# Agent attention and a gated feed-forward on one core: all products on two 64-row tiles of the matrix array, each with its own bank

## The chip, the cores and the metric

The kernel runs on one NeuronCore of a Trainium2 chip. The metric is the device time of one execution in microseconds (us). TensorE (PE in the profile) multiplies, ScalarE (ACT) and VectorE (DVE) read and write its result banks and do all elementwise work, GpSimd (POOL) and SyncE (SP) mostly issue transfers.

## What is computed

```python
def sm(a, b):                       # softmax of scaled products
    s = scale * (a @ b.transpose(0, 2, 1))
    s = s - s.max(-1, keepdims=True)
    e = np.exp(s)
    return e / (e.sum(-1, keepdims=True) + 1e-09)
agent_v = sm(agents, k) @ v         # 4 batches, 12480 keys, 49 agents, 128 channels
x = sm(q, agents) @ agent_v         # 49920 tokens, 128 channels
h = x @ w_in                        # w_in 128 x 2048
out = (h * (1 / (1 + np.exp(-1.702 * h)))) @ w_out
```

All data are float32. The weights arrive as 64-bit words and are turned into float32 on DVE.

## The kernel before

**Precision.** A product in full float32 is replaced by products of parts: each operand is split into a high part and the rest. The feed-forward uses float32r parts and drops the product of the two rests, so each product is three. The scores use three bf16 parts and six products.

**Work of one group.** The tokens are cut into 100 chunks of 500, two chunks to a group, 50 groups. `query_scores` multiplies the queries of a group with the 49 agents, a softmax follows, and `query_pairs` transposes its result. The second attention product is folded into the weights: per batch, `weights_part` makes `agent_v @ w_in`, so that the feed-forward takes the 49 softmax rows as its input. A group then has 16 steps, one for each 128 of the 2048 hidden features; `two_steps` records two steps at a time, 400 times in all.

**Up.** The softmax rows are held packed: 49 high rows, 49 rest rows and 30 of the 49 high rows again make 128 rows (`sa`, `sb`, one for each chunk), the remaining 19 rows lie apart in `rq`. So `up` issues four products on the whole array (L438: two hidden blocks by two chunks) and four on 32-row tiles of it (L441, 19 rows each), all into the four banks of `ph`. Eight small transfers for each group and up to six for each weight part (`move`) put the rows where this packing wants them.

**Gelu and split.** ACT applies the activation to each `ph` bank (L451). `high` makes the float32r part `gh`, by a casting transfer from POOL (L457), on ACT (L461) or, once in a group, on DVE (L459); `low` takes the rest on DVE (L466).

**Down.** Four steps later (`LAG = 4`) `down` multiplies with the second matrix (L476): three products for each of two chunks, each over 128 rows of the array, into the two banks of `po`, one for each chunk. After 16 steps `store` copies the banks out on ACT (L487) and SP sends them to memory.

**Order.** PE, ACT, DVE and POOL run in the order in which the program records them (`manual_schedule`). The skeleton of `two_steps`, with t an even step:

```python
g[t], g[t + 1] = up(...)          # PE, ACT
jobs(t)                           # attention work that is due at t
gh[t], gh[t + 1] = high(...)      # POOL, ACT or DVE
down(u = t - 3); second(t); down(u = t - 4)   # second(): jobs(t + 1), then one low()
if last step of the po banks: store(...)
```

Attention work is put at fixed steps: `query_pairs` at 4, `query_scores` at 12, the exponentials of the softmax at 0, key scores of the next batch (39 times in all) and its value products (39 times) at steps between. It has banks of its own, `ps_m`.

Of the kernel before, what the change touches and what calls it, by code (L numbers as in the profile page):

```python
# [8 lines left out]
F32 = mybir.dt.float32  # L9
# [10 lines left out]
KB = 8  # L20
# [17 lines left out]
R = 30  # L38
WORDS_USED = (3, 7, 11)
BOTH = (0,)  # L40
ON_DVE = (2,)
# [6 lines left out]
def kernel(  # L48
# [33 lines left out]
    ps_m = ctx.enter_context(tc.tile_pool(name="ps_m", bufs=2, space=bass.MemoryType.PSUM))  # L82


# [41 lines left out]
    def to_float32(w, out=None):  # L126
# [12 lines left out]
        m = work.tile([P, 512], U32, name="m21", tag="o")  # L139
# [50 lines left out]
    def scores(b, parts, ps, c):  # L190
        x0, x1, x2 = parts
        for j in range(c * KB // 2, (c + 1) * KB // 2):
            t = slice(j * TB, j * TB + P)
            o = ps[:, j * A : (j + 1) * A]
            products = [(x0, 0), (x0, 1), (x0, 2), (x1, 0), (x1, 1), (x2, 0)]
            for i, (x, y) in enumerate(products):
                nc.tensor.matmul(  # L197
                    out=o,
                    lhsT=x[:, t],
                    rhs=ag_part[:, b, y, :],  # L200
                    start=(i == 0),
                    stop=(i == len(products) - 1),
                )


    def score_halves(n, parts, c):
        x0, x1, x2 = parts
        b = chunk(n, c)[0]
        a = ag_part[:, b].rearrange("p i a -> p (i a)")
        mm = nc.tensor.matmul  # L210
        ps = ps_m.tile([P, 512], F32, name="ps_m")
        for j in range(KB // 2):
            t0 = (c * KB // 2 + j) * QB
            t = slice(t0, t0 + P)
            o = ps[:, j * 2 * A : (j + 1) * 2 * A]
            mm(out=o, lhsT=x0[:, t], rhs=a[:, 0 : 2 * A], start=True, stop=False)  # L216
            mm(out=o[:, A:], lhsT=x0[:, t], rhs=a[:, 2 * A :], start=False, stop=False)
            mm(out=o, lhsT=x1[:, t], rhs=a[:, 0 : 2 * A], start=False, stop=False)  # L218
            mm(out=o[:, 0:A], lhsT=x2[:, t], rhs=a[:, 0:A], start=False, stop=True)  # L219
        return ps[:QB, : KB * A].rearrange("p (j i a) -> p j a i", i=2, a=A)  # L220

    def score_bank():
        ps = ps_m.tile([P, 512], F32, name="ps_m")
        return ps, ps[:TB, : KB * A].rearrange("p (j a) -> p j a", a=A)
# [7 lines left out]
    def first_key_scores(g, kt):  # L232

        for c in range(2):
            ps = ps_m.tile([P, 512], F32, name="ps_m")
# [19 lines left out]
    def key_store(g, s):  # L255
        nc.scalar.copy(out=score[:TB, g * KB : (g + 1) * KB, :], in_=s)

# [5 lines left out]
    def key_max_1(d):  # L263
        mx = d["mx"]
        ps = ps_m.tile([P, 512], F32, name="ps_m")
# [3 lines left out]
        mrow = work.tile([P, TB], F32, name="mrow", bufs=1)  # L269
# [3 lines left out]
    def key_max_2(d):  # L273
        mrow = d["mrow"]
        ps = ps_m.tile([P, 512], F32, name="ps_m")
        nc.tensor.transpose(out=ps[:TB, :A], in_=mrow[:A], identity=ident[:A, :A])
        nc.vector.tensor_copy(out=max_b[:TB], in_=ps[:TB, :A])
# [31 lines left out]
    def key_matmuls(g, ps, first, last):  # L309
        for j in range(KB):  # L310
            nc.tensor.matmul(  # L311
                out=ps[:, : 2 * C + 2],
                lhsT=e_pair[g % 2][:TB, j, :],
                rhs=v_pair[:TB, j, :],
                start=(first and j == 0),
                stop=(last and j == KB - 1),
            )

    def key_values(g):
        ps = ps_m.tile([P, 512], F32, name="ps_m")  # L320
        key_matmuls(g, ps, True, True)
        return ps

    def key_sum(g, ps, acc):
        if g == 0:
            nc.vector.tensor_copy(out=acc, in_=ps[:, : 2 * C + 1])
        else:
            nc.vector.tensor_add(out=acc, in0=ps[:, : 2 * C + 1], in1=acc)


    def weights_0(acc, w):
        zc = work.tile([P, P], F32, name="zc", bufs=1)
        nc.vector.tensor_copy(out=zc, in_=acc[:, 2 * C : 2 * C + 1].broadcast_to([P, P]))
        w["acc"], w["zc"] = acc, zc

    def weights_1(w):
        ps = ps_m.tile([P, 512], F32, name="ps_m")
        nc.tensor.matmul(out=ps[:, 0:P], lhsT=w["acc"][:, 0:C], rhs=sel, start=True, stop=False)
        nc.tensor.matmul(out=ps[:, 0:P], lhsT=w["acc"][:, C : 2 * C], rhs=sel, start=False, stop=True)
        nc.tensor.matmul(out=ps[:, P : 2 * P], lhsT=w["zc"], rhs=sel, start=True, stop=True)  # L340
        rz = work.tile([P, P], F32, name="rz", bufs=1)
# [9 lines left out]
    def weights_part(b, w, c):  # L351
        if c == 0:
            wts[b] = wpool.tile([P, F], F32R, name="wh"), wpool.tile([P, F], F32R, name="wq")
        wh, wq = wts[b]
        s = slice(c * 512, (c + 1) * 512)
        pw = ps_m.tile([P, 512], F32, name="ps_m")
        nc.tensor.matmul(out=pw, lhsT=w["avT"], rhs=w_in_sb[:, s], start=True, stop=True)  # L357
        nc.scalar.copy(out=wh[:, s], in_=pw)
        wl = work.tile([P, 512], F32R, name="wl")
        nc.vector.tensor_sub(out=wl[:A], in0=pw[:A], in1=wh[:A, s].bitcast(F32))  # L360
        move(wh[A:H, s], wl[0 : R // 2])
        move(wh[H + A : P, s], wl[R // 2 : R])
# [489 lines left out]
```

## Time and profile before

| | |
|---|---|
| median of 3 runs | 1993.88 us (1993.75 to 1993.92) |
| profiled execution: its time | 1994.44 us |
| its span, first to last instruction | 1992.6 us |
| PE, DVE, ACT, POOL busy | 1954.5, 1628.2, 1425.9, 260.9 us |
| granted TensorE clock, mean | 0.990 |

Busy shares are means over the span. Matmuls overlap in the array, so their rows are best read by their starts: the distance from one start to the next is what a product costs. In the rows below `x2` joins two instructions that follow each other.

### The profile page before, as it was taken

Reading aid. Unit: us, or ns where it says so; the run is one execution under the profiler, and the core shown is the slowest. Engines: PE = TensorE matmul, PEld = TensorE weight load, DVE = VectorE, ACT = ScalarE, POOL = GpSimd, SP = SyncE. Lnnn points to the kernel's source line nnn. Section 1 sums busy time; section 2 is a strip of 40 time slices with the busy share of each in tenths; the row PEclk is TensorE's granted clock in tenths of the full one; section 3 lists DMA queues with packets and bytes.
Section 4 is the critical chain, followed back from the end, with each engine's and each line's share of the span. In section 5 each row is a group of like instructions: output and inputs, shape, how many; then the busy total and the mean of one; then the engine's idle time right before and its main releaser. Section 6 shows DMA issues by size and latency. Waiting matters only on the chain.

```text
span 1992.6 us, 33879 instructions
## 1 busy us (share of the span) xinstructions
PE 1954.5 (98%) x12462; PEld 1472.6 (74%) x12462; DVE 1628.2 (82%) x2081; ACT 1425.9 (72%) x2364; POOL 260.9 (13%) x597
## 2 busy tenths in 40 slices
PE   7799999999999999999999999999999999999999
PEld 7577777777777777777777777777777777777776
DVE  6689989988788889888878888988877767777775
ACT  3367777777767776777777777677677787777875
POOL 1111111111111111111111111111111111111111
PEclk8899999999999999999999999999999999999999
DMA  9556666566556665665546566565455454554543
GB/s 302 146 172 191 186 192 181 174 185 189 164 181 200 181 182 179 196 183 171 182 160 197 183 204 180 174 191 177 158 163 170 162 181 157 171 165 163 181 145 134
DMA packets 126537, 356.26 MB, mean 179 GB/s; under 512 B 15984, under 2 KB 54752, under 8 KB 126372
## 3 DMA queue, kind: packets, MB, share of 16 engines
q0 software_dynamic: 66080, 234.78, 35.9%
q1 hardware_dynamic: 60292, 119.33, 21.6%
q8 instruction: 98, 1.61, 0.3%
q14 instruction: 67, 0.55, 0.1%
HBM read 81.01 MB, written 25.56 MB: 53 GB/s over the span
## 4 chain that ended last, share of the span: by engine, by line
PE 88%; issue 6%; DVE 3%; DMA 1%; POOL 1%; ACT 1%; POOLq 0%; ACTq 0%; SPq 0%; DVEq 0%
PE po L476 52%; PE ph L438 17%; PE ph L441 8%; PE ps_m L197 2%; PE ps_m L311 2%; PE ps_m L411 1%; PE po L610 1%; PE ps_m L237 1%; PE ps_m L216 1%; PE ps_m L218 1%; DMA gh<-g 1%; DVE gl L466 1%; POOL gh L457 1%; PE ps_m L357 1%; PE ps_m L219 0%
## 5 line engine op out<-in xcount | busy, mean ns | idle before, releaser
L451 ACT ACTIVATE g<-ph 128x500 f32<-128x500 f32 x1600 | 811.1, 593 | 469.8 <-PE ph L441 463.5
L466 DVE TENSOR_TENSOR gl<-g,gh 128x1000 fp32r<-128x1000 f32 x800 | 940.1, 1196 | 129.6 <-DMA gh<-g 83.1
L476 PE MATMUL po<-gh,wo_h 128*128 128x500 f32 x1600 | 532.7, 414 | 0.0
L476 PE MATMUL po<-gl,wo_h 128*128 128x500 f32 x1600 | 494.7, 390 | 4.2 <-DVE gl L466 4.0
L476 PE MATMUL po<-gh,wo_l 128*128 128x500 f32 x1600 | 493.2, 389 | 0.0
L457 POOL DMA_DIRECT2D gh<-g x450 | 241.0, 535 | 1652.7 <-ACT g L451 1053.3
L476 PEld LDWEIGHTS po<-gl,wo_h 128*128 128x128 f32 x1600 | 300.3, 188 | 70.5 <-DVE gl L466 9.3
L476 PEld LDWEIGHTS po<-gh,wo_l 128*128 128x128 f32 x1600 | 301.9, 189 | 62.1
L476 PEld LDWEIGHTS po<-gh,wo_h 128*128 128x128 f32 x1600 | 272.4, 189 | 86.5 <-issue 55.1
L438 PE MATMUL ph<-sa,wh 128*128 128x500 f32 x800 | 315.8, 395 | 2.3 <-DMA wh<-wl 1.6
L461 ACT CAST gh<-g 128x1000 fp32r<-128x1000 f32 x300 | 309.5, 1032 | 8.8
L438 PE MATMUL ph<-sb,wh 128*128 128x500 f32 x800 | 314.7, 393 | 0.0
L441 PE MATMUL ph<-rq,wq 19*128 19x500 f32 x1600 | 201.5, 491 | 0.2 <-DMA wq<-wl 0.2
L438 PEld LDWEIGHTS ph<-sa,wh 128*128 128x128 f32 x800 | 151.3, 189 | 39.4 <-ACT g L451 7.7
L441 PEld LDWEIGHTS ph<-rq,wq 19*128 19x128 f32 x1600 | 76.8, 182 | 140.1 <-issue 139.2
L438 PEld LDWEIGHTS ph<-sb,wh 128*128 128x128 f32 x800 | 151.2, 189 | 38.2 <-ACT g L451 7.0
L186 DVE TENSOR_TENSOR rest<-rest 128x508 bf16<-128x508 f32 (+3 forms) x178 | 129.6, 737 | 0.9
L423 DVE TENSOR_TENSOR sa<-ps_m,sa 49x500 fp32r<-49x500 f32 x50 | 33.6, 672 | 48.2 <-ACT sb L421 48.0
L184 DVE TENSOR_TENSOR rest<-qt 128x508 f32<-128x508 f32 x100 | 67.6, 678 | 3.3 <-DMA qt<-qT 3.3
L487 ACT COPY o<-po 128x500 f32<-128x500 f32 x100 | 53.8, 606 | 13.6 <-PE po L476 13.2
L451 ACT ACT_TABLE_LOAD x49 | 62.9, 1283 | 0.9
L219 PE MATMUL ps_m<-ag_part,rest 128*128 128x49 bf16 x400 | 59.4, 186 | 3.7 <-DVE rest L186 3.7
(110 smaller groups left out, 1583.6 us busy)
## 6 DMA issues: line engine op xcount, KB each, us to landing
gh<-g POOLq DMA_DIRECT2D x450, 500.0 KB, 4.5
qt<-qT SPq DMA_DIRECT2D x100, 250.0 KB
kt<-kT SPq DMA_DIRECT2D x52, 480.0 KB
vt<-v SPq DMA_DIRECT2D x52, 480.0 KB
outT<-o SPq DMA_DIRECT2D x96, 250.0 KB
rq<-sa SPq DMA_DIRECT2D x100, 37.1 KB
rq<-sb SPq DMA_DIRECT2D x100, 37.1 KB
sa<-sa SPq DMA_DIRECT2D x100, 29.3 KB
```

The costliest lines, as they stand in the source:

```text
L184: nc.vector.tensor_sub(out=r[:, s], in0=t[:, s], in1=halves(t)[0][:, s])
L186: nc.vector.tensor_sub(out=halves(r)[1][:, s], in0=r[:, s], in1=halves(r)[0][:, s])
L197: nc.tensor.matmul(out=o, lhsT=x[:, t], rhs=ag_part[:, b, y, :], start=(i == 0), stop=(i == len(products) - 1),)
L219: mm(out=o[:, 0:A], lhsT=x2[:, t], rhs=a[:, 0:A], start=False, stop=True)
L438: nc.tensor.matmul(out=ph[k][:, :CH], lhsT=wts[c][0][:, cols[i]], rhs=pairs[c], start=True, stop=False)
L441: nc.tensor.matmul(out=ph[k][:, :CH], lhsT=wts[c][1][r, cols[i]], rhs=rq[r], start=False, stop=True, tile_position=(k * 32, 0),)
L451: nc.scalar.activation(out=gs[i][:, c, :], in_=ph[k][:, :CH], func=AF.Gelu_apprx_sigmoid)
L457: nc.gpsimd.dma_start(out=gh, in_=g)
L461: nc.scalar.copy(out=gh, in_=g)
L466: nc.vector.tensor_sub(out=gl, in0=g, in1=gh.bitcast(F32))
L476: nc.tensor.matmul(out=po[c][:, :CH], lhsT=lhsT[:, f, :], rhs=rhs[:, c, :], start=(begin and first), stop=(end and last),)
L487: nc.scalar.copy(out=o, in_=po[c][:, :CH])
```

## The change

Every product of the main loop is done in halves. The 128 rows of the array are used as two tiles of 64 rows (`on_rows(k, ...)`, k = 0 or 1), and the two tiles write into two banks.

- `up(c, e)` takes one chunk and two hidden blocks at a step. The tile k takes block 2e + k; each takes three products over 49 rows (high by high, high by the weights' rest, rest by high). The softmax rows lie in rows 0 to 48 and 64 to 112, so they are kept in two copies (`hi`, `lo`, and swapped in `hi2`, `lo2`, four transfers a group). The weight rest `wl` is a full tile and needs no transfers.
- `down` does the upper and lower 64 hidden features on the two tiles, so the two banks of `po` hold two halves of one chunk's sum. `store` copies both (one ACT copy of 128 x 1000), SP sends the first half to memory, and two steps on POOL sends the second half with an adding transfer (`store_add`). This happens every 8 steps.
- `scores` sends each of the six bf16 products as two of 64 rows, for keys and queries; `score_sum` adds the halves: a copy on ACT, then an addition on DVE. Before, the key scores needed the copy alone, and the query scores came from 32 products (four for each of 8 blocks of tokens), two columns of sums that DVE reduced straight from the banks.
- `key_values` and the transposes of `query_pairs` are halved too. `ps_m` is one buffer of two banks, where it was two buffers of one.
- The weight conversions stand in another order: three quarters of `w_in` before the loop, the last and all of `w_out` in its first steps (`LATER_WORDS`).
- The cast `gh` that DVE made once in a group (`ON_DVE`) goes to ACT.

```diff
+    def on_rows(k, n, out, lhsT, rhs, start, stop):
+        r = rows(k, n)
+        nc.tensor.matmul(out=out, lhsT=lhsT[r], rhs=rhs[r], start=start, stop=stop, tile_position=(k * H, 0))
...
-    def scores(b, parts, ps, c):
+    def scores(parts, places):
         x0, x1, x2 = parts
...
+        ps = two_banks()
+        products = [(x0, 0), (x0, 1), (x0, 2), (x1, 0), (x1, 1), (x2, 0)]
+        for j, (b, t0) in enumerate(places):
             for i, (x, y) in enumerate(products):
...
+                for k in range(2):
+                    on_rows(
+                        k, H, ps[:, k, j * A : (j + 1) * A], x[:, t0 : t0 + P], ag_part[:, b, y, :],
+                        i == 0, i == len(products) - 1,
+                    )
+        return ps
+
+    def score_sum(ps, n, out):
+        h = [ps[:n, k, : KB * A].rearrange("p (j a) -> p j a", a=A) for k in range(2)]
+        nc.scalar.copy(out=out, in_=h[0])
+        nc.vector.tensor_add(out=out, in0=h[1], in1=out)
...
-    def up(f, wts, pairs):
-        rq = pairs[2]
-        tiles = [(i, c) for i in range(2) for c in range(2)]
-        cols = [slice((f + i) * P, (f + i + 1) * P) for i in range(2)]
-        ph = [ps_h.tile([P, 512], F32, name="ph") for _ in tiles]
-        for k, (i, c) in enumerate(tiles):
-            nc.tensor.matmul(out=ph[k][:, :CH], lhsT=wts[c][0][:, cols[i]], rhs=pairs[c], start=True, stop=False)
-        for k, (i, c) in enumerate(tiles):
-            r = slice(k * 32, k * 32 + A - R)
-            nc.tensor.matmul(
-                out=ph[k][:, :CH],
-                lhsT=wts[c][1][r, cols[i]],
-                rhs=rq[r],
...
+    def up(c, e, wts, pairs):
+        wh, wl = wts
+        ph = [ps_h.tile([P, 512], F32, name="ph") for _ in range(2)]
+        for w, x, first, last in ((wh, 0, True, False), (wl, 0, False, False), (wh, 1, False, True)):
+            for k in range(2):
+                f = slice((2 * e + k) * P, (2 * e + k + 1) * P)
+                on_rows(k, A, ph[k][:, :CH], w[:, f], pairs[c != k][x], first, last)
...
-    def down(f, gh, gl, po, begin, end):
-        for lhsT, rhs, first, last in (
-            (wo_h, gh, True, False),
-            (wo_h, gl, False, False),
-            (wo_l, gh, False, True),
-        ):
-            for c in range(2):
-                nc.tensor.matmul(
-                    out=po[c][:, :CH],
-                    lhsT=lhsT[:, f, :],
-                    rhs=rhs[:, c, :],
...
+    def down(e, gh, gl, po, begin, end):
+        for w, x, first, last in ((wo_h, gh, True, False), (wo_h, gl, False, False), (wo_l, gh, False, True)):
+            for i in range(2):
+                for k in range(2):
+                    on_rows(
+                        k, H, po[:, k, :CH], w[:, 2 * e + i], x[:, i],
+                        begin and first and i == 0, end and last and i == 1,
+                    )
...
+    def store(m, po):
+        o = work.tile([P, 2, CH], F32, name="o", tag="o", bufs=1)
+        nc.scalar.copy(out=o, in_=po[:, :, :CH])
+        new, out = out_tokens(m)
+        nc.sync.dma_start(out=out, in_=o[:, 0, new:])
+        return o
+
+    def store_add(m, o):
+        new, out = out_tokens(m)
+        nc.gpsimd.dma_start(out=out, in_=o[:, 1, new:], accum_op=ALU.add)
```

PE between two attention jobs, kernel before: the up products of two steps (`sa`, `sb` packed rows on the whole array, `rq` the rest rows on four small tiles), then the down products of one step.

```order
L438 MATMUL ph<-sa,wh 128x500
L438 MATMUL ph<-sb,wh 128x500
L438 MATMUL ph<-sa,wh 128x500
L438 MATMUL ph<-sb,wh 128x500
L441 MATMUL ph<-rq,wq 128x500 x4
L476 MATMUL po_1969<-gh,wo_h 128x500
L476 MATMUL po_1970<-gh,wo_h 128x500
L476 MATMUL po_1969<-gl,wo_h 128x500
L476 MATMUL po_1970<-gl,wo_h 128x500
L476 MATMUL po_1969<-gh,wo_l 128x500
L476 MATMUL po_1970<-gh,wo_l 128x500
```

The same place in the changed kernel, where every row is on a 64-row tile (L91 is the helper `on_rows`): the up products of two steps, then the down products of one.

```order
L91 MATMUL ph<-hi_10616,wh 128x500
L91 MATMUL ph<-hi,wh 128x500
L91 MATMUL ph<-hi_10616,wl 128x500
L91 MATMUL ph<-hi,wl 128x500
L91 MATMUL ph<-lo_10617,wh 128x500
L91 MATMUL ph<-lo,wh 128x500
L91 MATMUL ph<-hi_10616,wh 128x500
L91 MATMUL ph<-hi,wh 128x500
L91 MATMUL ph<-hi_10616,wl 128x500
L91 MATMUL ph<-hi,wl 128x500
L91 MATMUL ph<-lo_10617,wh 128x500
L91 MATMUL ph<-lo,wh 128x500
L91 MATMUL po<-gh,wo_h 128x500 x4
L91 MATMUL po<-gl,wo_h 128x500 x4
L91 MATMUL po<-gh,wo_l 128x500 x4
```

Two steps held 4 + 4 + 12 products of 500 columns; now they hold 12 + 24, all of 64 rows or fewer.

ACT at the steps 0 to 4 of a group, kernel before: exponentials between two loads of the function table, the activations of step 2, the store copies, and the split of the transposed softmax (`sa`, `sb`).

```order
L390 ACT_TABLE_LOAD
L390 ACTIVATE e_sb<-e_sb 125x8x49
L451 ACT_TABLE_LOAD
L451 ACTIVATE g<-ph 128x500 x4
L487 COPY o<-po_11408 128x500
L487 COPY o<-po_11409 128x500
L451 ACTIVATE g<-ph 128x500 x4
L421 CAST sa<-ps_m 49x500
L421 CAST sb<-ps_m 49x500
L461 CAST gh<-g 128x1000
```

The same place in the changed kernel.

```order
L366 ACT_TABLE_LOAD
L366 ACTIVATE e_sb<-e_sb 125x8x49
L417 ACT_TABLE_LOAD
L417 ACTIVATE g<-ph 128x500 x4
L425 CAST gh<-g 128x1000
L449 COPY o<-po 128x1000
L417 ACTIVATE g<-ph 128x500 x4
L399 CAST hi<-ps_m 128x4x64
L399 CAST hi<-ps_m 128x4x61
L425 CAST gh<-g 128x1000
```

The cast that DVE made stands now on ACT ahead of the store copy, and the store is one copy of 1000 columns, which comes a second time at step 10 of each group.

## Rows read from the trace of the kernel before

**Rows 1.** The page: busy time and share of each engine; the ending chain by line.

```profile
PE 1954.5 (98%) x12462; PEld 1472.6 (74%) x12462; DVE 1628.2 (82%) x2081; ACT 1425.9 (72%) x2364; POOL 260.9 (13%) x597
...
PE po L476 52%; PE ph L438 17%; PE ph L441 8%; PE ps_m L197 2%; PE ps_m L311 2%; PE ps_m L411 1%; PE po L610 1%; PE ps_m L237 1%; PE ps_m L216 1%; PE ps_m L218 1%; DMA gh<-g 1%; DVE gl L466 1%; POOL gh L457 1%; PE ps_m L357 1%; PE ps_m L219 0%
```

**Rows 2.** Busy time in three stretches: length, engines, clock, DMA share, GB/s.

```profile
400.00:700.00 300.00, 299.33 (x2046) 224.63 (x2047) 253.79 (x322) 221.71 (x368) 39.58 (x89) 1.00 0.59 183
1000.00:1300.00 300.00, 297.83 (x2184) 224.91 (x2183) 262.48 (x341) 216.89 (x361) 38.95 (x91) 1.00 0.60 182
```

**Rows 3.** PE in order of time, one plain pair of steps: start, us, instruction.

```profile
1803.55 0.39 PE L438 MATMUL ph<-sa,wh 128*128 128x500 f32 x1
...
1804.23 0.38 PE L438 MATMUL ph<-sb,wh 128*128 128x500 f32 x1
1804.54 0.50 PE L441 MATMUL ph<-rq,wq 19*128 19x500 f32 x4
1804.97 0.73 PE L476 MATMUL po<-gh,wo_h 128*128 128x500 f32 x2
1805.54 0.61 PE L476 MATMUL po<-gl,wo_h 128*128 128x500 f32 x2
...
1807.81 0.39 PE L438 MATMUL ph<-sa,wh 128*128 128x500 f32 x1
```

**Rows 4.** PE in order of time, a pair of steps with key scores.

```profile
1100.61 0.39 PE L438 MATMUL ph<-sa,wh 128*128 128x500 f32 x1
...
1102.13 0.24 PE L197 MATMUL ps_m<-ag_part,rest 128*128 128x49 bf16 x3
...
1103.21 0.23 PE L197 MATMUL ps_m<-ag_part,rest 128*128 128x49 bf16 x3
1103.29 0.70 PE L476 MATMUL po<-gh,wo_h 128*128 128x500 f32 x2
1103.82 0.62 PE L476 MATMUL po<-gl,wo_h 128*128 128x500 f32 x2
...
1106.09 0.39 PE L438 MATMUL ph<-sa,wh 128*128 128x500 f32 x1
```

**Rows 5.** PE in order of time: where a pair of steps with query scores begins and ends.

```profile
1833.70 0.39 PE L438 MATMUL ph<-sa,wh 128*128 128x500 f32 x1
...
1839.10 0.38 PE L438 MATMUL ph<-sa,wh 128*128 128x500 f32 x1
```

**Rows 6.** PE in order of time, a pair of steps with the transposes.

```profile
1816.31 0.39 PE L438 MATMUL ph<-sa,wh 128*128 128x500 f32 x1
...
1817.74 0.65 PE L411 MATMUL ps_m<-ident,p_pad 125*128 125x125 f32 x4
1818.14 0.70 PE L476 MATMUL po<-gh,wo_h 128*128 128x500 f32 x2
...
1820.94 0.39 PE L438 MATMUL ph<-sa,wh 128*128 128x500 f32 x1
```

**Rows 7.** ACT in order of time, steps 0 to 4 of a group.

```profile
907.91 2.02 ACT L451 ACTIVATE g<-ph 128x500 f32<-128x500 f32 x4 [1.19 <-PE ph L441]
...
913.83 2.03 ACT L451 ACTIVATE g<-ph 128x500 f32<-128x500 f32 x4
915.72 1.09 ACT L487 COPY o<-po 128x500 f32<-128x500 f32 x2
916.87 2.03 ACT L451 ACTIVATE g<-ph 128x500 f32<-128x500 f32 x4
```

**Rows 8.** PE in order of time, steps 4 and 5 of the same group, to the next up.

```profile
914.88 0.39 PE L438 MATMUL ph<-sa,wh 128*128 128x500 f32 x1
915.11 0.39 PE L438 MATMUL ph<-sb,wh 128*128 128x500 f32 x1
915.43 0.50 PE L438 MATMUL ph<-sa,wh 128*128 128x500 f32 x1
915.91 0.50 PE L438 MATMUL ph<-sb,wh 128*128 128x500 f32 x1
...
919.97 0.39 PE L438 MATMUL ph<-sa,wh 128*128 128x500 f32 x1
```

**Rows 9.** Groups of instructions, shapes apart: count, busy us, mean ns, idle before.

```profile
L461 ACT CAST gh<-g 128x1000 fp32r<-128x1000 f32 x300 | 309.5, 1032 | 8.8
...
L381 DVE TENSOR_REDUCE e_sb<-ps_m 125x196 f32<-125x392 f32 x100 | 52.5, 561 | 1.5 <-PE ps_m L219 0.8
...
L459 DVE CAST gh<-g 128x1000 fp32r<-128x1000 f32 x50 | 34.0, 679 | 22.0 <-ACT g L451 22.0
...
L253 DVE TENSOR_TENSOR run_max<-score,run_max 120x392 f32<-120x392 f32 x48 | 27.1, 565 | 38.9 <-ACT score L256 32.0 <-ACT score L246 6.7
...
L256 ACT COPY score<-ps_m 120x392 f32<-120x392 f32 x39 | 18.6, 478 | 0.0
```

**Rows 10.** Waits: who waited for whom, us in total, times, longest.

```profile
PEld ph L438 <- ACT g L451: 14.7, 48, 1.2
...
PEld po L476 <- DVE gl L466: 9.3, 13, 3.0
```

**Rows 11.** The startup: a wait of PE in the first steps.

```profile
99.21 2.07 PE L357 MATMUL ps_m<-w_in_sb,avT 128*128 128x512 f32 x2 [7.14 <-DVE w_in_sb L146]
```

**Rows 12.** DMA issues of the page: count, KB each, us to landing.

```profile
gh<-g POOLq DMA_DIRECT2D x450, 500.0 KB, 4.5
```

More of the change, by code (lines that the diff above doesn't have):

```diff
@@ L346, in weights_1, with weights_part @@
         w["avT"] = avT
-    def weights_part(b, w, c):
+    def weights_part(b, w, c, n=1):
         if c == 0:
[L353 to L357, printed above, removed]
-        nc.scalar.copy(out=wh[:, s], in_=pw)
[L359 to L362, printed above, removed]
-        for i in range(4):
-            move(wq[i * 32 : i * 32 + A - R, s], wl[R:A], None if b or c else nc.gpsimd)
-    def move(out, in_, queue=None):
-        (queue or nc.sync).dma_start(out=out.bitcast(F32), in_=in_.bitcast(F32))
+            wts[b] = wpool.tile([P, F], F32R, name="wh"), wpool.tile([P, F], F32R, name="wl")
+        wh, wl = wts[b]
+        s = slice(c * 512, (c + n) * 512)
+        pw = two_banks()[:, 0:n]
+        for i in range(n):
+            t = slice((c + i) * 512, (c + i + 1) * 512)
+            nc.tensor.matmul(out=pw[:, i], lhsT=w["avT"], rhs=w_in_sb[:, t], start=True, stop=True)
+        pw = pw.rearrange("p n f -> p (n f)")
+        nc.scalar.copy(out=wh[:, s], in_=pw)
+        nc.vector.tensor_sub(out=wl[:, s], in0=pw, in1=wh[:, s].bitcast(F32))
     def query_load(n):
@@ new lines, in query_pairs @@
+        ps = two_banks()
+        hi, lo, hi2, lo2 = (work.tile([P, CH], F32R, name=x) for x in ("hi", "lo", "hi2", "lo2"))
+        parts = []
+        for k, n in enumerate((H, QB - H)):
+            for i in range(KB // 2):
+                nc.tensor.transpose(
+                    out=ps[:, k, i * n : (i + 1) * n],
+                    in_=pp[rows(k, n), i, :],
+                    identity=ident[rows(k, n), rows(k, n)],
+                    tile_position=(k * H, 0),
+                )
+            t = [x.rearrange("p (i t) -> p i t", t=QB)[:, :, rows(k, n)] for x in (hi, lo)]
+            parts.append((ps[:, k, : KB // 2 * n].rearrange("p (i t) -> p i t", t=n), *t))
@@ L527, in do_query_split, with do_key_scores @@
             pieces[n](i)
-    def do_key_scores(b, g, c):
-        if c == 0:
-            banks[b, g] = score_bank()
-        scores(b, k_parts[b, g], banks[b, g][0], c)
+    def do_key_scores(b, g):
+        banks[b, g] = scores(k_parts.pop((b, g)), [(b, j * TB) for j in range(KB)])
     def do_key_store(b, g):
-        key_store(g, banks.pop((b, g))[1])
+        score_sum(banks.pop((b, g)), TB, score[:TB, g * KB : (g + 1) * KB, :])
     def do_key_values(b, g):
@@ L641, in ahead @@
     def ahead(n):
[L642 to L643 removed]
+        do_query_scores(n)
         do_query_load(n + 1)
@@ L670 @@
     pe_steps = {n * NF + f for n in range(NG) for f in (Q_AT, P_AT)}
-    due = [b * CB // 2 * NF for b in range(B)]
+    due = [b * CB * NF // 2 for b in range(B)]
     def put(t, fn):
@@ L796, in two_steps @@
             second(t, f)
-        elif e == NF - 2:
-            store(m, po.pop(m))
+        elif e == NF // 2 - 2:
+            put(t + 3, lambda m=m, o=store(m, po.pop(m)): store_add(m, o))
     def second(t, f):
@@ L812 @@
             two_steps(t)
+        for t in range(steps + LAG, steps + LAG + 2):
+            jobs(t)
     assert not at
```

218 lines of the change are left out of this document (77 added, 141 removed).

## The prediction

> **What bounds the kernel now.** The page comes first: PE is busy 98% of the span, DVE 82%, ACT 72%, and the chain that ended last is PE's own down and up products for more than three quarters [rows 1]. The windows say the same of the middle: in 300 us PE idles 0.7 to 2.2 us at the full granted clock (1.00 of the 2.4 GHz level), and DVE is busy 85 to 87% [rows 2]. The waits of PE for others are small: 14.7 us for ACT's activations, 9.3 us for DVE's rests, in the whole run [rows 10]. So the time is the sum of what PE's products cost, and a busy share can't show that; the starts can.
>
> Two steps without attention work take 1807.81 - 1803.55 = 4.26 us [rows 3]. From the second down pair to the next up, ten products of 500 columns take 2.27 us, 0.227 us each. At 2.4 GHz 500 columns are 0.208 us, so 0.019 us of each is handing over. The rest is around the four small tiles: from the last whole-array up product to them 0.31 us, from them to the first down product 0.43 us, and the first two down products 0.57 us where two others take 0.454 [rows 3]. The small tiles start together and count as one slot, so 0.08 + 0.20 + 0.12 = 0.40 us of the 4.26 go to leaving the whole array and coming back. Check: 17 slots of 0.227 and 0.40 are 4.26.
>
> **Feed-forward.** The change replaces 4 whole products, one slot of small tiles and 12 whole products by 12 + 24 products on 64 rows. If the two tiles run side by side this is 18 slots, one more than before, and the 0.40 us is gone because all of the loop has one tiling. The trace has no 64-row tile. The nearest row is the four 32-row tiles: four products of 500 columns, their weight loads included, leave room for the next after 0.43 us, where one after another they would take 0.83 [rows 3]. So tiles run side by side, load side by side and write several banks at once. I take a pair at the price of a whole product, 0.227: 18 x 0.227 = 4.09, a gain of 0.17 us, times 400 **-70 us**. Below it is bounded by the 500 columns, 0.208 (-206 us); above by one tile after the other, 0.454 (+1564). One nanosecond of the pair is 7,200 x 1 ns = 7.2 us, and the gain is gone at 4.26 / 18 = 0.2367.
>
> **Scores.** Two steps with key scores take 5.48 us, 1.22 over the plain ones; 42 products take 1.08 us, 25.7 ns each [rows 4]. With query scores they take 5.40, 1.14 over [rows 5]. Now both have 48 pairs. If a pair costs what one product costs, 48 x 25.7 ns = 1.23 us, and the first two down products behind them take 0.53 instead of 0.454 [rows 4], which was hidden in the 0.40 before. That is 1.31 for each: 39 x 0.09 + 50 x 0.17 = **+12 us**. Above: each half costs 25.7 ns on its own, 89 x 1.23 = 109 us more.
>
> **Transposes and values.** Four transposes take 0.40 us, their pair of steps 4.63, 0.37 over the plain ones [rows 6]. Now there are eight, four on one tile, then four on the other: between 0.40 (hidden beside each other) and 0.80. In order they can overlap only where one tile's last meets the other's first, and the columns are half; I take 0.65, with 0.08 for the first down products 0.73, 50 x 0.36 = **+18 us** (5 to 26). The value products become as many pairs as they were products, at nothing if pairs run side by side as above.
>
> **Whole-array work left.** 17 attention jobs in the loop (eight of `weights_part`, three of `weights_1`, six of `key_max`) still use 128 rows. Each pays the 0.40 of leaving and coming back [rows 3]: **+7 us** (0 to 7).
>
> **ACT and DVE.** ACT gets 50 casts of 1.03 us from DVE's L459, 50 copies of query scores of 0.48, and 100 stores of some 1.03 (the cast of the same shape) [rows 9]. DVE loses the 50 casts (34 us) and 100 reduces (52 us) and gets 89 additions of some 0.565 (50 us) [rows 9]. With PE at 1968 us both keep room, 89% of DVE in the heavy stretch [rows 2]; that room is the cover. One place has none: steps 0 to 4, where ACT holds exponentials and two table loads, 3.9 us between the activations of step 0 and those of step 2 [rows 7]. PE there waits already, the products of its up at 914.88 get 0.32 and 0.48 us apart, and the stretch is 5.09 long instead of the 4.63 with the transposes alone [rows 6, 8]. The cast that DVE made is put on ACT ahead of the store copy, so the copy ends some 1.0 us later. Late next are the down products of step 4, which need the `po` banks; up and transposes (1.36 + 0.65 us) cover most. Of at most 1.03 in each of the 18 groups that have key exponentials I take a third, **+6 us** (0 to 19).
>
> `store_add` waits on POOL for the first half's landing. Behind it queue the casting transfers `gh`, for which DVE and then PE wait. It is issued two steps after the copy, and a transfer of twice the size lands in 4.5 us [rows 12], about the length of two steps, so I cost it at nothing; if the cover is gone, each us is 100 us in all at worst. The single `o` buffer is needed again eight steps later, four times that landing. SP's fewer small transfers gain nothing: their rows are read twelve steps after the transposes, which covers them before and after.
>
> **Startup and end.** In the first group PE waits 7.14 us for the last quarter of `w_in` [rows 11]. It is converted sooner now, but the down weights are due at twice the rate, on the same DVE: between -7 and +7, I take **-4 us**. At the end a second transfer follows the first: **+4 us** (0 to 4.5, the landing above).
>
> **Sum**, against the profiled execution's 1994.44 (span 1992.6 and 1.8 around it, 0.56 over the median): -70 + 12 + 18 + 7 + 6 - 4 + 4 = -27, 1967.4, and 1966.9 by the median. I say **1967**.
>
> **Rivals.**
>
> *The handing over shrinks (0.20).* If the 0.019 us between products overlap between two tiles, a pair comes near its columns, 0.213: 7,200 x 0.014 = -101 us, 1866. DVE would then be needed 93% of the heavy stretch and give some of it back: about 1880. For it: nothing in the rows says that the handing over is per tile. Against it: the whole-array products show it wherever the columns are 500.
>
> *Each half of a score costs its own slot (0.15), slower.* It decides from 32 ns for a pair of 49 columns on, where 89 x 48 x 6.3 ns takes the 27 us back. At 51 ns a pair it is +109 us, 2076; half of that is 2022. For it: 25.7 ns are more than the 20.4 of 49 columns at 2.4 GHz, so something else may set them. Against it: four small tiles started as one row [rows 3]. The Trainium skill (TensorEngine Tiling (Array Packing), Performance Considerations) gives each matmul an overhead of about 60 cycles and advises against a tiling factor taken from a dimension that is small already; 60 cycles at 2.4 GHz are, as an estimate from that page, 25 ns, the rows' 25.7, and by that rule this rival holds. No row here shows two such halves side by side.
>
> *More waits of ACT and DVE (0.14), slower.* `score_sum` makes DVE wait for a copy on ACT that stands behind a cast, 89 times, the `ps_m` buffer is single, and the store comes twice a group. DVE waited 0.8 us on average for such a copy (38.9 us in 48) [rows 9]. If half of it and of the 1.03 of each store reach PE, it is 36 + 52 us: about 2050; 2010 if a quarter does.
>
> *Nothing gained (0.08).* At 0.231 a pair the sum is +2: 1996, within 0.2% (4 us, about what a measurement of this kernel can tell).
>
> *No weight load behind a running product (0.06).* Then each pair carries its load: the small tiles' 0.43 holds one load, the columns and the leaving, so a pair would be 0.43 less the 0.10 or so of leaving, 0.33: 7,200 x 0.10 = +740 us, 2710. The whole-array rows speak against it, since their load is hidden in the 0.227 [rows 3]. The Trainium skill (TensorE: Matmul & The Clock Gate, Part 3) says that a load overlaps a running matmul only where the row groups differ; by that rule this rival holds, but the whole-array products in the trace already break it.
>
> **How the numbers follow.** The likeliest case keeps 0.37, its own range 1940 to 1990 (2 ns of the pair either way and the bounds of the transposes and of ACT). The five rivals have the rest. The range leaves out the last rival, and the far ends of the first three: 1880 to 2060. Faster by over 0.2%: likeliest 0.36 and first rival 0.20, 0.56. Within: 0.09. Slower: 0.35.
>
> **What would show it.** Down and up products of one tile 0.227 us apart, the other tile's beside them; two plain steps 4.09; no 0.4 us gap by a change of tiling outside the 17 jobs; key and query scores 1.3 us over the plain steps, the transposes 0.73. DVE's additions waiting less than 1 us for ACT, and PE's waits for `po` and `ph` at step 4 below 1 us. It is wrong if the pairs lie outside 0.223 to 0.233, if scores take over 1.8 us, or if PE's waits for DVE or ACT exceed 50 us.

## The result, and the profile after

The changed kernel takes 1974.73 us (median of 4 runs, 1971.15 to 1977.17), the kernel before in the same job 1993.9. The ratio is 0.9902, 95% interval 0.9885 to 0.9919: faster by 1.0%, where 1.4% was forecast. The profiled execution takes 1976.1 us, 18.3 less than the one of before.

The page of the changed kernel, to be held against [rows 1]:

```profile
PE 1912.4 (97%) x24458; PEld 1704.4 (86%) x24458; DVE 1554.4 (79%) x2017; ACT 1507.0 (76%) x2460; POOL 353.2 (18%) x693
...
PE 75%; ACT 8%; DVE 8%; issue 6%; DMA 2%; POOL 0%; POOLq 0%; ACTq 0%; DVEq 0%; SPq 0%
```

PE has twice the products and is busy 42 us less, DVE 74 us less, ACT 81 us more. ACT holds 8% of the ending chain, where it held 1%.

PE of the changed kernel in order of time, one plain pair of steps, as [rows 3] (`x2` is one pair, a product on each of the two tiles, and `x4` two pairs):

```profile
1802.14 0.40 PE L91 MATMUL ph<-hi,wh 49*128 49x500 f32 x2
...
1803.28 0.41 PE L91 MATMUL ph<-lo,wh 49*128 49x500 f32 x2
1803.50 0.64 PE L91 MATMUL po<-gh,wo_h 64*128 64x500 f32 x4
1803.96 0.64 PE L91 MATMUL po<-gl,wo_h 64*128 64x500 f32 x4
...
1806.21 0.43 PE L91 MATMUL ph<-hi,wh 49*128 49x500 f32 x2
```

Two steps take 4.07 us where they took 4.26. From 1802.14 to 1806.21 there are 18 pairs at even distances, 0.226 us, and the gaps of [rows 3] around the four small tiles (0.31, 0.43 and 0.57 us) are gone. A pair of half products costs what a whole product cost.

The same distance, from one first up product to the next, over groups 2 to 49, in us (medians):

| two steps with | before | after | foretold |
|---|---|---|---|
| no attention work | 4.254 | 4.083 | 4.09 |
| key scores | 5.486 | 5.424 | 5.40 |
| query scores | 5.371 | 5.407 | 5.40 |
| value products | 5.218 | 5.040 | - |
| transposes, no wait | 4.64 | 4.39 | 4.82 |
| transposes, 16 groups (4, 12, 24, 36 to 48) | 4.64 | 4.76 | 4.82 |
| transposes, 18 groups with key exponentials | 5.10 | 5.54 | 5.62 |

The last two lines hold new waiting: 0.37 us over the pairs without a wait in the 16 groups, and 0.44 more than before in the 18, although the transposes themselves cost 0.25 less.

ACT of the changed kernel, steps 0 to 4 of a group with key exponentials, as [rows 7]:

```profile
869.22 1.28 ACT L417 ACT_TABLE_LOAD   x1
870.52 2.03 ACT L417 ACTIVATE g<-ph 128x500 f32<-128x500 f32 x4
872.57 1.03 ACT L425 CAST gh<-g 128x1000 fp32r<-128x1000 f32 x1
873.51 0.98 ACT L449 COPY o<-po 128x1000 f32<-128x1000 f32 x1
```

PE at the same place, as [rows 8]:

```profile
871.84 0.44 PE L91 MATMUL ph<-hi,wh 49*128 49x500 f32 x2
...
873.26 0.52 PE L390 MATMUL ps_m<-ident,p_pad 64*128 64x64 f32 x8
874.54 0.72 PE L91 MATMUL po<-gh,wo_h 64*128 64x500 f32 x4 [0.76 <-ACT o L449]
...
877.38 0.39 PE L91 MATMUL ph<-hi,wh 49*128 49x500 f32 x2
```

The last product into `po` was issued before 871.84. Its copy could have run at once, but ACT is at the activations that the exponentials delayed, and then at the cast that came from DVE. The copy ends at 874.49 and PE goes on at 874.54.

A second new wait stands in three groups (5, 17, 29; called the late query scores below), whose pair of steps with the query scores takes 8.8 to 8.9 us (6.77 before). PE in group 17:

```profile
776.43 0.25 PE L91 MATMUL ps_m<-ag_part,qt 64*128 64x49 bf16 x6 [0.59 <-DVE acc L308]
...
778.33 0.22 PE L91 MATMUL ps_m<-ag_part,rest 64*128 64x49 bf16 x2 [0.98 <-DVE rest L194]
...
779.13 1.18 PE L91 MATMUL po<-gh,wo_h 64*128 64x500 f32 x4
780.11 1.04 PE L91 MATMUL po<-gl,wo_h 64*128 64x500 f32 x4
780.94 1.00 PE L91 MATMUL po<-gh,wo_l 64*128 64x500 f32 x4
```

First the single `ps_m` buffer has to be read by DVE, then the rest of the queries' split is late on DVE. The long products behind these waits stand 0.415 us apart for some 2.6 us: the windows of this stretch (length, busy time of PE, PEld, DVE, ACT, POOL, clock, DMA share, GB/s) show the granted clock at 0.50, the 1.2 GHz level:

```profile
772.00:776.00 4.00, 3.85 (x34) 2.88 (x32) 3.97 (x6) 2.68 (x5) 0.03 (x1) 1.00 0.58 173
776.00:779.10 3.10, 1.68 (x96) 1.60 (x98) 3.06 (x6) 2.47 (x5) 0.54 (x2) 0.88 0.98 334
779.10:781.70 2.60, 2.60 (x22) 2.17 (x18) 2.53 (x5) 0.49 (x1) 0.86 (x1) 0.50 0.60 140
```

At the end the last product stands at 1964.4, 9.9 us before the end of the span, where it was 4.6: ACT copies both halves, one transfer lands, then POOL issues the adding one:

```profile
1968.46 0.86 POOL L456 DMA_DIRECT2D outT<-o  x1 [10.59 <-DMA outT<-o]
```

### The profile page after: what moved, and what is told of

It is laid out like the page before. It is cut to its first block, busy times and chain, and to the rows that moved or that the text cites. A ratio compares the mean times of both kernels' runs of the same rounds, so it can differ in the third digit from the quotient of the medians.

```text
span 1974.3 us, 57475 instructions
## 1 busy us (share of the span) xinstructions
PE 1912.4 (97%) x24458; PEld 1704.4 (86%) x24458; DVE 1554.4 (79%) x2017; ACT 1507.0 (76%) x2460; POOL 353.2 (18%) x693
## 4 chain that ended last, share of the span: by engine, by line
PE 75%; ACT 8%; DVE 8%; issue 6%; DMA 2%; POOL 0%; POOLq 0%; ACTq 0%; DVEq 0%; SPq 0%
PE po L91 46%; PE ph L91 21%; PE ps_m L91 6%; ACT g L417 4%; DVE gl L430 3%; ACT o L449 1%; DMA gh<-g 1%; ACT L417 1%; ACT L366 1%; PE ps_m L342 1%; DVE v_pair L294 1%; PE ph L227 1%; ACT e_sb L366 0%; DVE v_pair L293 0%; DVE rest L194 0%
## 5 line engine op out<-in xcount | busy, mean ns | idle before, releaser
L91 PE MATMUL po<-gh,wo_h 64*128 64x500 f32 x3200 | 529.1, 396 | 15.3 <-ACT o L449 14.0
L91 PE MATMUL po<-gl,wo_h 64*128 64x500 f32 x3200 | 516.5, 388 | 7.6 <-DVE gl L430 7.6
L91 PE MATMUL po<-gh,wo_l 64*128 64x500 f32 x3200 | 513.9, 386 | 0.0
L91 PEld LDWEIGHTS po<-gl,wo_h 64*128 64x128 f32 x3200 | 333.6, 185 | 48.6 <-DVE gl L430 16.2
L91 PEld LDWEIGHTS po<-gh,wo_l 64*128 64x128 f32 x3200 | 335.3, 185 | 34.7 <-issue 0.4
L91 PEld LDWEIGHTS po<-gh,wo_h 64*128 64x128 f32 x3200 | 320.4, 186 | 50.6 <-ACT o L449 19.9
L91 PE MATMUL ph<-hi,wh 49*128 49x500 f32 x1600 | 337.9, 389 | 7.1 <-ACT g L417 6.3
L91 PE MATMUL ph<-hi,wl 49*128 49x500 f32 x1600 | 337.9, 387 | 0.0
L91 PE MATMUL ph<-lo,wh 49*128 49x500 f32 x1600 | 337.7, 387 | 0.0
L91 PEld LDWEIGHTS ph<-hi,wh 49*128 49x128 f32 x1600 | 174.5, 185 | 30.1 <-ACT g L417 8.3
L91 PEld LDWEIGHTS ph<-hi,wl 49*128 49x128 f32 x1600 | 174.1, 187 | 18.3 <-issue 1.5
L91 PEld LDWEIGHTS ph<-lo,wh 49*128 49x128 f32 x1600 | 174.4, 185 | 16.6
L91 PE MATMUL ps_m<-ag_part,rest 64*128 64x49 bf16 x4272 | 122.7, 182 | 3.5 <-DVE rest L194 3.5
L91 PEld LDWEIGHTS <-rest 64*128 64x128 bf16 x4272 | 113.4, 94 | 4.0 <-DVE rest L194 3.9
L456 POOL DMA_DIRECT2D outT<-o x100 | 87.6, 876 | 99.7 <-DMA outT<-o 87.2
```

The costliest lines, as they stand in the source:

```text
L91: nc.tensor.matmul(out=out, lhsT=lhsT[r], rhs=rhs[r], start=start, stop=stop, tile_position=(k * H, 0))
L456: nc.gpsimd.dma_start(out=out, in_=o[:, 1, new:], accum_op=ALU.add)
```

## The experiments

All start from the changed kernel ("after" below, 1974.7 us) except where said. The cuts of code show the lines that matter. Ratios are to the kernel before, with 95% intervals.

### The change of tiling

`down` on the whole array again, into one bank (so the copy of the second half and the adding transfer go too):

```diff
             for i in range(2):
-                for k in range(2):
-                    on_rows(k, H, po[:, k, :CH], w[:, 2 * e + i], x[:, i], ...)
+                nc.tensor.matmul(out=po[:, 0, :CH], lhsT=w[:, 2 * e + i], rhs=x[:, i], ...)
```

> The changed kernel with one thing undone: down multiplies on all 128 rows into one bank, so the transfer that adds the halves and the second half of the copy go. Up, scores, values and transposes stay on 64 rows. The number of slots stays at 18 for two steps, but the loop leaves the 64-row tiling and comes back once in two steps. Theory: this change of tiling costs what it cost before, 0.40 us, so two plain steps take 4.08 + 0.40 = 4.48 us, and the time is 1975 + 400 x 0.40 - 5 (no second transfer at the end) = about 2130 us. Rival: the 0.40 us belonged to the 32-row products and their loads, not to a change of tiling: two plain steps stay at 4.08 and the time at about 1970. Second rival: a pair of halves is cheaper or dearer than a whole product: then the products of down inside the stretch lie away from 0.227 us; at 0.222 it would be 12 x 5 ns x 400 = 24 us less.

Only the first pair of each `down` as one product of 128 rows:

```diff
+                if first and i == 0:
+                    nc.tensor.matmul(out=po[:, 0, :CH], lhsT=w[:, 2 * e], rhs=x[:, 0], start=begin, stop=False)
+                    continue
```

> The changed kernel with the first pair of each down replaced by one product on all 128 rows (two of 36 slot entries in two steps, apart from each other); all else is on 64 rows. Theory: what costs is each leaving and coming back, whatever lies between: twice in two steps, 2 x 0.40 = 0.80 us, 4.88 us for two plain steps and about 1975 + 320 = 2295 us. Rival: the cost goes with the number of whole-array products (here 2, with the whole down 12): less than half of what the whole down costs, under 2060 us. Second rival: no cost, 1975 us.

Measured: 2073.9 us (ratio 1.040, 1.038 to 1.042) and 2238.1 us (1.122, 1.120 to 1.124). Two plain steps take 4.474 and 4.875 us: 0.39 and 0.79 over after. PE of the version with the whole `down`:

```profile
1856.50 0.62 PE L436 MATMUL po<-gh,wo_l 128*128 128x500 f32 x2
1857.05 0.49 PE L91 MATMUL ph<-hi,wh 49*128 49x500 f32 x2
1857.38 0.38 PE L91 MATMUL ph<-hi,wl 49*128 49x500 f32 x2
...
1858.28 0.40 PE L91 MATMUL ph<-lo,wh 49*128 49x500 f32 x2
1858.61 0.72 PE L436 MATMUL po<-gh,wo_h 128*128 128x500 f32 x2
1859.16 0.61 PE L436 MATMUL po<-gl,wo_h 128*128 128x500 f32 x2
```

Changing the tiling costs twice 0.10 us: 0.55 instead of 0.45 for the last two products before it, 0.33 instead of 0.227 for the first pair behind it; and the same on the way back (1858.28 to 1858.61, 1858.61 to 1859.16). Inside a stretch both kinds stand 0.227 us apart. Twelve whole products in one stretch cost 0.39, two in two stretches 0.79: it goes by the changes, not by the products. The theory holds for each pair of steps. It failed for the sum: 99 and 263 us in place of 155 and 320. With the whole `down` the steps' starts behind the first group say where the rest is: the 204 plain pairs of steps lose 75 us, the 39 with values 16 and the 85 with scores 18, but the 48 with transposes gain 9, and the six with two parts of the weights lose nothing. The pairs with transposes take 4.78 us in all but a few groups, where after has 5.54 in those with key exponentials: a slower PE hides ACT's lateness, so what one step loses is not to be multiplied by 400.

### The halves of the scores

```diff
-                for k in range(2):
-                    on_rows(k, H, ps[:, k, j * A : (j + 1) * A], ...)
+                nc.tensor.matmul(out=ps[:, 0, j * A : (j + 1) * A], lhsT=x[:, t0 : t0 + P], ...)
...
-        nc.vector.tensor_add(out=out, in0=h[1], in1=out)
```

> The changed kernel with the six score products on all 128 rows into one bank; the addition of the halves on DVE is gone (a copy on ACT is left). Theory: two halves side by side cost what one product costs, so the products' own time stays at about 1.25 us for 48, and leaving the 64-row tiling costs some 0.35 more in each of 89 jobs: two steps with key scores 5.42 + 0.35 = 5.77 us, time 1975 + 31 - 3 (late rests of DVE) = about 2003 us, 1995 to 2010. Rival: each half has a cost of its own that the mean hides, so whole products save more than the change of tiling costs: 1975 us or less.

Measured: 1990.5 us (0.998, 0.997 to 0.999), 16 over after; two steps with key scores take 5.646, 0.22 more. PE of after, then of this version, from the first to the last key score:

```profile
1093.37 0.27 PE L91 MATMUL ps_m<-ag_part,kt 64*128 64x49 bf16 x4
...
1094.62 0.47 PE L91 MATMUL po<-gh,wo_h 64*128 64x500 f32 x1
1094.63 0.20 PE L91 MATMUL ps_m<-ag_part,rest 64*128 64x49 bf16 x2
```

```profile
1103.80 0.42 PE L91 MATMUL ph<-lo,wh 49*128 49x500 f32 x2
1104.16 0.25 PE L204 MATMUL ps_m<-ag_part,kt 128*128 128x49 bf16 x3
...
1105.33 0.23 PE L204 MATMUL ps_m<-ag_part,rest 128*128 128x49 bf16 x3
1105.49 0.73 PE L91 MATMUL po<-gh,wo_h 64*128 64x500 f32 x4
```

The first and last of the 48 products start 1.226 us apart, the 48 pairs 1.280 (medians of 35 pairs of steps): 1.1 ns more for each pair, not 25. That difference lies at the ends of the stretch; over 40 slots in its middle a pair and a whole product both stand 25.8 ns apart. Taking the halves back saves 0.05 us and pays 0.27 for leaving and coming back around these small products, less than around the long ones. The theory holds in direction; the price of the tiling change here was expected at 0.35.

### The cast of step 3

Back on DVE, with its rest and place in the order as before the change:

```diff
+ON_DVE = (2,)
...
+        elif f - 1 in ON_DVE:
+            nc.vector.tensor_copy(out=gh, in_=g)
...
-            (late if e in BOTH else after).append(t - 1)
+            (late if e in BOTH else lows if e in ON_DVE else after).append(t - 1)
```

> The changed kernel with one thing undone: the cast of step 3 of each group is on DVE again, as before the change, and its rest and its place in the order too. Theory: ACT's lateness at steps 2 to 4 costs 17 us (0.69 in 17 groups with key exponentials, 0.37 in 13 of the last groups), and the cast of 1.04 us ahead of the store copy is the cause: 1958 to 1965 us, the pair of steps with the transposes in the groups of the exponentials 5.5 -> about 4.9 us. Rival: the store copy itself makes the lateness: 1972 to 1976. Second rival: DVE, with 34 us more, gets late elsewhere and eats it: 1972 to 1985.

Measured: 1953.4 us (0.979, 0.978 to 0.981), 21 less than after. The steps' starts give 22.8, and 23.2 of it is in the pairs of steps with the transposes: 17.1 in the 18 groups with key exponentials (5.54 to 4.47 in most), 6.1 in the 16 others. Nothing else moves, although DVE has 34 us more. ACT and PE of this version, at the same place of the same group:

```profile
860.67 2.03 ACT L418 ACTIVATE g<-ph 128x500 f32<-128x500 f32 x4
862.56 1.03 ACT L452 COPY o<-po 128x1000 f32<-128x1000 f32 x1
863.43 2.08 ACT L418 ACTIVATE g<-ph 128x500 f32<-128x500 f32 x4
```

```profile
863.41 0.41 PE L391 MATMUL ps_m<-ident,p_pad 64*128 64x64 f32 x6
863.64 0.49 PE L92 MATMUL po<-gh,wo_h 64*128 64x500 f32 x1
863.66 0.29 PE L391 MATMUL ps_m<-ident,p_pad 61*128 61x61 f32 x2
863.76 0.70 PE L92 MATMUL po<-gh,wo_h 64*128 64x500 f32 x3
```

The copy stands right behind the activations, ends at 863.6, and the first product into `po` starts at 863.64, on one tile, while the other still transposes. At 4.47 us these pairs have lost not only the new wait but also the one that the kernel before had here (5.09 against 4.63 [rows 6, 8]).

Is it ACT, or the order of the rests that this edit moves too? The cast stays on ACT, only the order is changed:

```diff
+ON_DVE = (2,)
...
-            (late if e in BOTH else after).append(t - 1)
+            (late if e in BOTH else lows if e in ON_DVE else after).append(t - 1)
```

> The changed kernel with one thing changed: the cast of step 3 stays on ACT, but its rest is taken on DVE ahead of the attention work of step 4 instead of behind it, as in the version with the cast on DVE. Theory: the 21 us of that version come from ACT being free for the store copy, not from the order: 1970 to 1985 us, and the transposes' pair of steps in the groups of the exponentials stays at 5.3 to 5.6 us. Rival: the order brings it: 1953 to 1960 us.

Measured: 1975.7 us (0.990, 0.988 to 0.992), no gain; 5.50 to 5.57 in most of the 18 groups. It is ACT. The cast by a transfer, on neither engine:

```diff
-BOTH = (0,)
+BOTH = (0, 2)
```

> The changed kernel with the cast of step 3 of each group made by a casting transfer from POOL (as steps 0 and 1 have it), so neither ACT nor DVE makes it; its rest follows two steps later. Theory: what the cast on DVE gave back (1974.7 to 1953.4 us) came from ACT being free for the store copy at steps 2 to 4, and DVE's 34 us were hidden but for the late query splits: 1945 to 1954 us, the transposes' pair of steps in the groups of the exponentials about 4.4 to 4.5 us. Rival: the gain came from the place in the order (the rest of step 3 ahead of the attention work), so without DVE's cast and with the rest two steps later it does not come: over 1965 us. Second rival: the transfer lands late and DVE and PE wait for it, 1 us in each group: over 1995 us.

Measured: 1960.3 us (0.983, 0.981 to 0.985). The transposes' pair of steps falls to 4.45 to 4.53 in most of the groups, so the theory's cause is right: the gain comes with ACT free, whoever makes the cast. The time is missed by 6 us. In a dozen places PE waits 0.3 to 1.3 us more than with DVE's cast, the three late query scores are 1.5 us shorter each, and 4 us are the startup of the profiled run, for which no cause was tried.

### The same cast in the kernel before

The kernel before, with its `ON_DVE = (2,)` emptied:

> The kernel before with one part of the change alone: its cast of step 3 goes from DVE to ACT. Theory: ACT's lateness at steps 2 to 4 is a matter of this cast and shows without 64-row tiles too, but smaller, since the transposes and the up products there cover 0.17 us more and the store copies come once in a group: some 0.5 us in each of the 18 groups with key exponentials, the pair of steps with the transposes there 5.09 -> 5.6 us: 2003 us (1996 to 2010). Rival: only the two stores in a group of the changed kernel bring it: 1994, no change.

Measured: 2054.6 us (1.030, 1.028 to 1.031), seven times the expected loss. The foreseen place shows what was foretold, 5.10 to 5.64 us in the 18 groups (10 us). Most of the other 50 us come two or four steps later, some 1.0 us in nearly every group: in group 2 two steps with key scores go from 5.48 to 6.51. DVE and PE of this version there:

```profile
183.12 0.65 DVE L184 TENSOR_TENSOR rest<-kt 128x480 f32<-128x480 f32 x1
185.32 0.67 DVE L423 TENSOR_TENSOR sa<-ps_m,sa 49x500 fp32r<-49x500 f32 x1 [1.54 <-ACT sb L421]
186.00 0.68 DVE L423 TENSOR_TENSOR sb<-ps_m,sb 49x500 fp32r<-49x500 f32 x1
186.70 1.20 DVE L466 TENSOR_TENSOR gl<-g,gh 128x1000 fp32r<-128x1000 f32 x1
187.81 0.69 DVE L186 TENSOR_TENSOR rest<-rest 128x480 bf16<-128x480 f32 x1
```

```profile
188.56 0.20 PE L197 MATMUL ps_m<-ag_part,rest 128*128 128x49 bf16 x1 [0.86 <-DVE rest L186]
```

Without `ON_DVE` the rest of step 3 is recorded behind the transposes' rests, DVE stands idle in order until ACT has copied the transposes out, and the key split behind both is late. In the whole run DVE waits 149.5 us for these copies, 48.0 in the kernel before. So the theory missed a second wait that the same edit makes, of DVE for ACT in the order of the program. The cast's time and the order were not tried apart in this kernel.

### The adding transfer

The halves of the output are added on DVE, and the adding transfer is left out:

```diff
-        nc.scalar.copy(out=o, in_=po[:, :, :CH])
+        nc.scalar.copy(out=o[:, 0], in_=po[:, 0, :CH])
+        nc.vector.tensor_add(out=o[:, 0], in0=po[:, 1, :CH], in1=o[:, 0])
...
-        nc.gpsimd.dma_start(out=out, in_=o[:, 1, new:], accum_op=ALU.add)
```

> The changed kernel with the output's halves added on chip: ACT copies the first half (128x500), DVE adds the second to it, one transfer stores the sum; no adding transfer. Theory: the adding transfer costs nothing in the loop (POOL's waits of 87 us are hidden) and some 5 us at the end, and DVE's 100 additions of some 0.6 us stand in order behind a copy that ends 0.7 us after PE's last product, so DVE loses some 1 us in each of 100 places, most of it in its spare time: -5 at the end, 0 to +20 in the groups with key work: 1970 to 1990 us. Rival: POOL's waits delay the casts and cost 10 us and more: then 1965 us or less.

Measured: 1994.5 us (1.000, 0.999 to 1.001), 20 over after and 4 over the theory's upper end. Waits of PE and of DVE in this version:

```profile
PE po L91 <- DVE o L452: 31.6, 48, 1.1
```

```profile
DVE o L452 <- ACT o L451: 100.7, 54, 2.8
```

PE waits 31.6 us for the addition, where after has 14.0 for the copy. POOL's 87.2 us of waiting for the first landing in after were hidden: without them the plain pairs of steps stay at 4.083 us. Only the end is 4.8 us shorter. Against this addition, which stands on DVE behind a copy on ACT, the adding transfer is worth 1%.

### Putting it together

The cast on DVE, the last store alone added on DVE, and the query splits two steps earlier:

```diff
-S_AT = 8
+S_AT = 6
...
+        if m == 2 * NG - 1:
+            nc.scalar.copy(out=o[:, 0], in_=po[:, 0, :CH])
+            nc.vector.tensor_add(out=o[:, 0], in0=po[:, 1, :CH], in1=o[:, 0])
```

> The changed kernel with three edits: the cast of step 3 on DVE (measured: 1953.4), the query splits two steps earlier (at steps 6 to 9), and only the last store added on DVE with one transfer. Theory: at three groups the query scores wait 0.6 us for the addition of the value sums and 1.0 us for the split and run 4 us at half clock after that, 3.4 us each; two steps earlier the split's wait is gone, and half of the rest: -5 to -8 us. The last store: -4 to -5 us. Together 1941 to 1945 us. Rival: DVE is behind in these groups, and what is moved ahead makes the value sums later by the same: only the end is gained, 1949 us.

Measured: 1964.0 us (0.985, 0.983 to 0.986), 11 slower than the cast on DVE alone. The three late query scores are gone (5.5 us now), and the end is 5.1 us, but in 18 groups PE now waits at steps 8 and 9:

```profile
887.72 0.72 PE L92 MATMUL po<-gl,wo_h 64*128 64x500 f32 x4 [1.08 <-DVE gl L433]
```

That is 1.2 us in each, 22 us. The split's pieces now stand on DVE ahead of the rests that `down` needs at step 8. Neither the theory nor its rival had this: what was moved ahead made something else late, in six times as many groups.

The splits back at their steps, the cast and the last store kept on DVE, and the 13 value products of a batch shared otherwise:

```diff
-V_SLOTS = (3, 2, 2, 2, 2, 2)
+V_SLOTS = (2, 2, 2, 2, 2, 3)
```

> The changed kernel with the cast of step 3 on DVE (1953.4 measured), the last store alone added on DVE with one transfer, and the 13 value products of a batch shared 2, 2, 2, 2, 2, 3 over six groups, where it was 3 first; the query splits stay at steps 8 to 11. Theory: the end gives 5 us (the last product stood 10.1 us ahead of the span's end, 5.0 with the one transfer in the run with the earlier splits), and the three late query scores of 8.8 to 8.9 us come from three value products, the split and the score shifts on DVE in one group; in the sixth group the shifts are done, so they fall to about 5.5: -10 us. 1938 us, 1934 to 1943. Rival: the third value product alone makes DVE late, and the wait only moves to the sixth group: 1948 us. Second rival: the weights that follow the values come too late or wait: over 1953 us.

Measured: 1944.8 us (0.975, 0.974 to 0.977), 7 above the theory, 3 below its rival. The query scores of groups 5, 17 and 29 take 5.4 us, those of the sixth groups with values (10, 22, 34) 6.65, so 6.5 us of the ten are won: part of the wait has moved there with the third value product, as the rival said. The end is won too:

```profile
core 0 of [0], span 1943.3 us
...
1938.02 0.63 PE L92 MATMUL po<-gh,wo_l 64*128 64x500 f32 x4
```

This version beats both kernels, by 2.5% and 1.5%.

## Why the prediction was right, point by point

The sum was -27 us, 18.3 were measured between the profiled executions, and the terms that are read from the steps' starts give -21; the other 3 us are not assigned (medians stand for many steps, and executions of the changed kernel differ by up to 6 us). The largest term was right in its mechanism and its size. That the total came so near is in part luck: the transposes were taken 22 us too dear and ACT 11 us too cheap.

| term | foretold | measured | from |
|---|---|---|---|
| feed-forward | -70 | -68 | 400 x (4.083 - 4.254) |
| scores | +12 | +15 | 39 x 0.109 + 50 x 0.208 over the plain steps |
| transposes | +18 | -4 | 50 x (0.31 - 0.39) |
| ACT at steps 2 to 4 | +6 (0 to 19) | +17 | 27.8 - 11.0, all time over 4.39 and 4.64 in 48 pairs of steps |
| whole-array jobs | +7 | +6 | 17 jobs |
| late query splits | none | +6 | 3 x (8.84 - 6.77) |
| startup | -4 | +2 | first group |
| end | +4 | +5 | 9.9 - 4.6 |

**Feed-forward.** The step holds: 0.2268 us a pair against 0.227, and its two halves (the handing over of 0.019 us stays; the 0.40 of the tiling goes) are shown by the two versions with whole products, where the 0.40 comes back as 0.39 for each leaving and coming back. (They change between 64 rows and the whole array; that the change to 32 rows in the kernel before cost the same is argued from the equal size.) The first rival, a cheaper pair, is out, and so is the last, the load that no product hides: on each tile 0.208 of the 0.227 us are columns, and the load takes 185 ns in the mean (page, costliest groups), so it lies behind the running product of the same tile:

```profile
L91 PEld LDWEIGHTS po<-gl,wo_h 64*128 64x128 f32 x3200 | 333.6, 185 | 48.6 <-DVE gl L430 16.2
```

By the Trainium skill (TensorE: Matmul & The Clock Gate, Part 3) a load overlaps a running product only where the row groups differ; the text above that list also lets a load into the background weight buffer go ahead. The trace does not agree with the list, for halves as for the whole array (185 and 189 ns of load beside 0.208 us of columns within 0.227 us).

**Scores.** 1.34 us where 1.31 was foretold. The rival that each half costs a slot is out: 1.1 ns a pair, by the run with whole scores. The Trainium skill (TensorEngine Tiling (Array Packing), Performance Considerations) gives each matmul an overhead of about 60 cycles; if the second half of each pair paid it too, that would be, as an estimate from that page, 25 ns more, and the run does not agree (1.1 ns).

**Transposes.** This step failed in size: 0.31 us over the plain steps, not 0.73. The sum put eight at 0.65 us and 0.08 behind them. On one tile they start 60 ns apart (medians of 59 to 63 in the version with DVE's cast), where those of 125 rows mostly stood 107 ns apart, and the tiles overlap at both ends: the second tile's first starts 0.11 us before the first tile's last, and the next down product of the first tile starts before the second tile's last transposes (863.64 above, and so in each of the 47 groups from group 2 on), which the sum of four and four left out.

**ACT.** The step named the place, the late copy and the late down products rightly, but took a third of 1.03 us in 18 groups. PE's waits at this place grew by 17 us, 16 groups without key exponentials among them, and taking the cast from ACT removes 23. What failed is the cover: the transposes that were to hide the copy are 0.42 us shorter than the sum said, and PE waits in their place. So the two errors are one and nearly cancel: these pairs of steps take 4.76 and 5.54 us where the sum had 4.82 and 5.62.

**DVE.** `score_sum` waits longer than foretold, 84.1 + 35.8 us, 1.35 on average over the 89 additions where less than 1 was expected, but little of it reaches PE (all waits of PE for ACT and DVE come to 44 us in the run, under the 50 that the prediction set), so the third rival's path was real and its share was not a quarter. What reaches PE from DVE is the split in three groups, which no step named.

**POOL and the end.** The wait of `store_add` costs nothing in the loop, as said, and 5 us at the end; the adding transfer lands in 5.5 us where 4.5 was taken from the casting one.

**Startup.** The sign failed: +2 us for -4. The wait of 7.14 us for `w_in` [rows 11] is gone, but two others came, for activations and for rests (6.4 of the 7.6 us in the first group):

```profile
PE ph L91 <- ACT g L417: 6.3, 1, 6.3
PE po L91 <- DVE gl L430: 7.6, 6, 4.5
```

The activations stand on ACT behind a cast of the second matrix, `wo_h`, which waits 3.9 us for DVE's conversion. That is the load on DVE that the term named, at more than its middle.

## What to carry to other kernels

Count the changes of tiling in a loop before counting products: here one out and back cost 0.39 us, as much as 1.7 products of 500 columns, and a loop that stays on one tiling can afford an extra slot. When PE gets faster, read which engine was hidden behind it, and where: here the pair of steps with the late copy of the result banks gave back a quarter of the 68 us, and one cast put on the other engine returned it. Judge a move in an ordered queue by what stands behind it, not by the engine's mean load.

## What the runs showed of the hardware

Two 64-row tiles run side by side without any loss at 500 columns: 0.2268 us for a pair, 0.227 for a whole product. At 49 columns both stand 25.8 ns apart, and a stretch of 48 pairs is 0.05 us longer than one of 48 whole products. The halves write two banks at once: each pair of `down` goes into both banks of `po` within its 0.2268 us. A tile may begin long products while the other still transposes (863.64 against 863.66) or still multiplies scores (1094.62 against 1094.63), out of the order in which the program records them. A change between 64-row tiles and the whole array costs 0.20 us each way around products of 500 columns. Behind waits of 0.6 and 1.0 us, 1.9 us from one to the other, the granted clock stood at 0.50, and long products stood 0.415 us apart for some 2.6 us: each of the three places took 3.4 us more than the other query scores, 1.6 of them waiting. An adding transfer of 250 KB from POOL lands in 5.5 us, against 3.5 for the casting one of 500 KB.
